# Attention beside a 2D Fourier filter on one core: queue order from an event simulation, exps over three and two PSUM banks in turn

## The chip, the cores and the metric

One core of one Trainium2 chip. The metric is the device time in microseconds of one execution; the time shown for a kernel is the median of several runs.

## The reference

Two independent parts share an input shape of 2048 x 640 and are written side by side (2048 x 1280, bf16).

Part A: a 2D real FFT of `A_x`, multiplied by a complex filter, and transformed back.

Part B: multi-head attention with 32 heads of 20 columns each:

```python
qkv = (x @ wqkv).reshape(B, S, 3, H, Dh).transpose(2, 0, 3, 1, 4)   # H = 32, Dh = 20
p = softmax(einsum("bhqd,bhkd->bhqk", q, k) * Dh ** -0.5)
o = einsum("bhqk,bhkd->bhqd", p, v).transpose(...).reshape(B, S, D) @ wo
```

## The kernel before, in words

**Tiles.** A head has only 20 columns, so four heads are packed on TensorE: a group `g` of four heads (8 groups) and a query block `qc` of 512 rows (4 blocks) make one of 32 units. A unit has 16 key chunks of 128 rows x 4 heads = 64 score tiles of 128 x 512; all 32 units have 2048. A score tile is one matmul with 20 contraction rows (`emit_qk`, L1550); up to four such matmuls run side by side in the rows of the array. ScalarE then takes the exponential of several tiles in one instruction, from PSUM to SBUF in bf16 (`emit_exp`, L1560). The result multiplies V with a column of ones appended (21 columns per head, `emit_pv`, L1589), and the four heads of a unit accumulate side by side in PSUM bank 6; the ones column gives the softmax denominators.

**PSUM.** Banks 0 to 2 and 3 to 5 are two halves of three tiles each. One exp reads a half (1536 columns) while TensorE fills the other. Bank 6 is the accumulator, bank 7 the single bank for all other work.

**Unit end** (`unit_done`). VectorE copies bank 6 to SBUF (L1603), four DMAs spread the denominators (L359 is the helper for all DMAs, issued by SyncE), VectorE takes the reciprocal (L1609), one DMA writes it to DRAM, one reads it back broadcast to all partitions, and GpSimd multiplies (L1615). When the eight units of a query block are done, eight out-projection jobs of eight matmuls each follow (L1633).

**Background jobs.** Part A is a chain of small matmul stages (L1115, L1148, L1168, L1192, L1224, L1288, L1314), with a pointwise stage on GpSimd (L1253 to L1258). The K projection (L1481), Q projection (`job_QA`, L1503) and V projection (L582) belong to part B. Each job is a run of matmuls into one PSUM bank and one evacuation to SBUF (L226 on VectorE, L225 on ScalarE; ScalarE evacuates only until the first scores).

**Order.** The engines take their instructions in program order, and a planner writes that order. `run` walks through steps of `T_STEP` = 1440 ns. Each step emits one exp, one score group of three tiles, one PV group of up to four tiles, and background matmuls for what is left of the step:

```python
budget = T_STEP - 250.0 * n_qk - 80.0 * n_pv - 150.0
banks = [7]
```

All costs are those of TensorE at its full clock. `unit_done` queues the whole unit end at once, the reciprocal directly behind the copy and the normalize behind it; the out-projection becomes due eight steps later.

Of the kernel before, what the change touches and what calls it, by code (L numbers as in the profile page):

```python
# [263 lines left out]
class KB:  # L264
# [805 lines left out]
    def mk_jobs_A(self, p0_after):  # L1070
# [205 lines left out]
        for lt in range(3):  # L1276
            M = 128 if lt < 2 else 65
            for sp in range(8):
# [16 lines left out]
                ev = [(mkev, 490.0, 598.0, [], [("ZT", lt, sp)] + zw("C", 2), [])]  # L1295
# [54 lines left out]
T_STEP = 1440.0  # L1350


class FK(KB):

# [5 lines left out]
    def alloc(self):  # L1360
# [22 lines left out]
        self.rin = [a.f32(take(64), 16) for _ in range(2)]  # L1383
        self.rall = a.f32(take(2048), 512)
# [5 lines left out]
        self.kron = a.bf(take(768), 3 * 128).rearrange("p (m k) -> p m k", m=3)  # L1390
        self.ws = self.osb[1].bitcast(BF16)[:, 0:656]
        self.zone(off[0], total)

    def zone(self, z, total):
# [9 lines left out]
        zA, zB, zC, zK = self.zA, self.zB, self.zC, self.zK  # L1404
        self.Wn = a.bf(zA, 2 * 16 * 328).rearrange("p (c k l) -> p c k l", c=2, k=16)
# [18 lines left out]
    def setup_B(self):  # L1424
        P = self.P
        nc = self.nc
# [4 lines left out]
        self.dma(self.xBn[:, 0:4, :], xB[:, 0:4, :], w=[("xBn", 0)], name="ld_xB0")  # L1431
        self.dma(self.wqkv[:, :, 640:720], wv[:, :, 640:720], w=[("wqkv", "k0")], name="ld_wk0")
        self.dma(self.wqkv[:, :, 0:80], wv[:, :, 0:80], w=[("wqkv", "q0")], name="ld_wq0")
        self.dma(self.xBn[:, 4:8, :], xB[:, 4:8, :], w=[("xBn", 1)], name="ld_xB1")
        self.dma(self.wqkv[:, :, 1280:1920], wv[:, :, 1280:1920], w=[("wqkv", 1)], name="ld_wv")
        for i in range(2, 4):
            self.dma(self.xBn[:, 4 * i:4 * i + 4, :], xB[:, 4 * i:4 * i + 4, :], w=[("xBn", i)], name="ld_xB%d" % i)
        self.dma(self.wqkv[:, :, 720:1280], wv[:, :, 720:1280], w=[("wqkv", "k")], name="ld_wk")
        self.dma(self.wqkv[:, :, 80:640], wv[:, :, 80:640], w=[("wqkv", "q")], name="ld_wq")
        wq, wk = self.wq_pad, self.wk_pad  # L1440
        ws = self.ws
        P.add("dve", lambda e: e.memset(ws, 0.25), w=[("ws",), ("osb", 1)], name="ms_ws")
        P.add("act", lambda e: e.activation(ws[:, 640:648], ws[:, 0:8], AF.Exp), r=[("ws",), ("osb", 1)], w=[("ws2",)], name="act_warm")
# [8 lines left out]
        wo = self.wo_pad.rearrange("p g n -> p (g n)")  # L1452
        P.add("pool", lambda e: e.memset(wo, 0.0), w=[("woz",)], name="ms_wo")
        o1 = self.ones1
        P.add("pool", lambda e: e.memset(o1, 1.0), w=[("ones1",)], name="ms_ones")
        wod = self.B_wo.rearrange("(g j d) n -> j d g n", g=8, j=4)
        for j in range(4):
            self.dma(self.wo_pad[32 * j:32 * j + 20, :, :], wod[j], r=[("woz",)], pw=[("wo",)], name="ld_wo%d" % j)
        for g in range(NG):
            for which, dst, key in ((1, wk, "wk"), (0, wq, "wq")):  # L1460
# [4 lines left out]
                if g < 1:  # L1465
                    P.add("act", (lambda d4, src: lambda e: e.copy(d4, src))(d4, src), r=[skey] + zk, w=[(key, g)], name="wpad")
                else:
                    P.add("pool", (lambda d4, src: lambda e: e.tensor_copy(d4, src))(d4, src), r=[skey] + zk, w=[(key, g)], name="wpad")

    def mk_jobs_B_static(self):  # L1470
        jobs = KB.mk_jobs_B_static(self)
        for g in range(NG):
            for kc in range(4):
                pe = []
                for cbv in range(5):
                    def mk(bank, cbv=cbv, g=g, kc=kc):
                        o = self.ps[:, bank, :]
# [5 lines left out]
                jobs[("K", g, kc)].pe = pe  # L1483
        return jobs

    def dummy(self, bank, n=512):
        ps = self.ps
        l = self.ws[:, 0:128]
        r_ = self.ws[:, 128:128 + n]
        self.P.add("pe", lambda e: e.matmul(ps[:, bank, 0:n], l, r_, start=True, stop=True),  # L1490
                   r=[("ws",), ("osb", 1)], w=[("ps", bank)], name="dummy")

    def job_QA(self, u):
# [17 lines left out]
        cond = (lambda p, u=u: self.qk_unit > u - 2) if u >= 2 else None  # L1511
        return Job("QA%d" % u, 2.0 + 32.0 * u - 6.0, pe, ev, after=[self.sj[("xT", qc, gi)] for gi in range(3)], cond=cond)


    def tile_of(self, t):
        u, w = divmod(t, 64)
        kt, j = divmod(w, 4)
        qc, g = divmod(u, NG)
        return u, qc, g, kt, j

    def group(self, i):
        return range(3 * i, min(3 * i + 3, self.ntiles))

    def qk_ready(self, p, i):
        for t in self.group(i):
            u, qc, g, kt, j = self.tile_of(t)
            for J in (self.qa_jobs.get(u), self.sj[("K", g, kt // 4)]):
                if J is None or J.done_p is None or J.done_p > p:
                    return False
        h = i % 2  # L1530
        for J in self.inflight:
            if J.bank in (3 * h, 3 * h + 1, 3 * h + 2):
                return False
        return True

    def emit_qk(self, i):
        ps, kt_ = self.ps, self.KT
        tiles, rk, wk = [], [], []
        for n, t in enumerate(self.group(i)):
            u, qc, g, kt, j = self.tile_of(t)  # L1540
            bank = 3 * (i % 2) + n
            tiles.append((j, g, kt, self.QA[u % 2], bank))
            rk += [("QA", u % 2), ("KT", g, kt // 4)]
            wk.append(("ps", bank))
            self.qk_unit = u
# [17 lines left out]
    def emit_pv(self, p):  # L1563
# [19 lines left out]
        if not tiles:  # L1583
            return 0
# [266 lines left out]
```

## Time and profile before

| | us |
|---|---|
| median of three runs (1208.11 to 1226.37) | 1223.77 |
| the profiled execution, its own time | 1226.82 |
| its span, first to last instruction | 1225.0 |
| ScalarE busy, 78% of the span | 951.9 |
| TensorE busy, 83% of the span | 1014.8 |
| VectorE busy, 20% | 246.0 |
| GpSimd busy, 11% | 137.6 |

PE is TensorE, PEld its weight loads, ACT ScalarE, DVE VectorE, POOL GpSimd, SPq the queue of SyncE. Busy time counts an instruction from its start to its modelled end; neighbours overlap, so the distance between starts says more than a mean duration. PEclk is the granted clock of TensorE: 1.00 is 2.4 GHz, 0.50 is 1.2 GHz, and a value between them is a mean over a stretch that had both.

### The profile page before, as it was taken

How to read it: one execution, taken by the hardware profiler on the slowest of the kernel's cores; microseconds unless marked ns; L12 is line 12 of the kernel's file. 1: busy time of each engine (PE TensorE's matmuls, PEld its weight loads, DVE VectorE, ACT ScalarE, POOL GpSimd, SP SyncE). 2: the span in 40 equal slices, each digit the busy share in tenths (PEclk: the TensorE clock that was granted, in tenths of full speed). 3: DMA queues.
4: the chain of work that ended last, by engine and by line, in shares of the span. 5: the costliest groups of instructions: out<-in, count | busy, mean ns of one | idle time of the engine just before them, and what ended most of it. 6: DMA issues, size and time to landing. Idle time of an engine off the chain costs nothing.

```text
span 1225.0 us, 13302 instructions
## 1 busy us (share of the span) xinstructions
PE 1014.8 (83%) x5818; PEld 291.8 (24%) x5864; DVE 246.0 (20%) x439; ACT 951.9 (78%) x689; POOL 137.6 (11%) x123
## 2 busy tenths in 40 slices
PE   7888888988869988897888788988888868888884
PEld 3322322223323212211112222223211211111112
DVE  3222333113212222331111233112100100000002
ACT  3678897977777977877778676757999869999990
POOL 4000001100000000273533000000000000000000
PEclk7788997557888666856557766559655755556556
DMA  6000003030000100000002000101000000000001
GB/s 194 1 10 11 9 1 99 10 123 10 10 26 6 62 10 10 1 10 10 10 8 88 15 10 2 40 31 52 23 10 10 25 15 10 10 10 10 10 10 33
DMA packets 30664, 31.85 MB, mean 26 GB/s; under 512 B 12936, under 2 KB 25864, under 8 KB 30216
## 3 DMA queue, kind: packets, MB, share of 16 engines
q1 hardware_dynamic: 30600, 30.94, 8.0%
q8 instruction: 47, 0.77, 0.3%
q14 instruction: 17, 0.14, 0.0%
HBM read 25.16 MB, written 5.51 MB: 25 GB/s over the span
## 4 chain that ended last, share of the span: by engine, by line
PE 52%; ACT 30%; DVE 6%; DMA 6%; SPq 3%; issue 2%; POOL 1%
ACT arena L1560 30%; PE ps L1550 12%; PE ps L1589 11%; DVE arena L226 4%; PE ps L1633 4%; PE ps L1503 4%; PE ps L1481 4%; PE ps L1314 3%; SPq L359 3%; DMA arena<-arena 3%; PE ps L1168 2%; PE ps L1224 2%; PE ps L582 2%; DMA arena<-rscr 2%; PE ps L1288 2%
## 5 line engine op out<-in xcount | busy, mean ns | idle before, releaser
L1560 ACT ACTIVATE arena<-ps 128x1536 bf16<-128x1536 f32 (+1 forms) x683 | 947.7, 1497 | 234.4 <-PE ps L1550 209.0
L1550 PE MATMUL ps<-arena 20*128 20x512 bf16 x2048 | 357.6, 517 | 61.2 <-ACT arena L1560 57.7
L1589 PE MATMUL ps<-arena 128*21 128x512 bf16 x2048 | 356.4, 517 | 5.6 <-DVE arena L1603 1.9
L226 DVE CAST arena<-ps 128x320 bf16<-128x320 f32 (+4 forms) x291 | 167.0, 574 | 623.6 <-PE ps L1503 167.1
L1615 POOL TENSOR_TENSOR arena<-arena 128x512 bf16<-128x512 f32 x32 | 40.5, 1265 | 1037.5 <-DMA arena<-rscr 1037.5
L1550 PEld LDWEIGHTS ps<-arena 20*128 20x128 bf16 x2048 | 69.7, 96 | 350.0 <-ACT arena L1560 217.0
L1589 PEld LDWEIGHTS ps<-arena 128*21 128x21 bf16 x2048 | 66.7, 91 | 249.2 <-issue 232.3
L1633 PE MATMUL ps<-arena 128*128 128x320 bf16 x256 | 52.7, 346 | 46.0 <-POOL arena L1615 45.5
L1481 PE MATMUL ps<-arena 128*128 128x512 bf16 x149 | 51.6, 451 | 19.6 <-DVE arena L226 17.0
L1503 PE MATMUL ps<-arena 128*128 128x512 bf16 x135 | 55.3, 511 | 7.7 <-issue 6.5
L226 DVE COPY arena<-ps 128x1024 bf16<-128x1024 bf16 (+2 forms) x57 | 35.5, 623 | 89.8 <-PE ps L1115 64.7
L1603 DVE COPY arena<-ps 128x512 f32<-128x512 f32 x32 | 22.1, 692 | 140.8 <-PE ps L1589 140.5
L1224 PE MATMUL ps<-arena 128*128 128x512 bf16 (+1 forms) x78 | 33.6, 514 | 20.0 <-DVE arena L226 14.1
L1314 PE MATMUL ps<-arena 128*128 128x320 bf16 (+1 forms) x192 | 43.0, 374 | 7.5 <-DVE arena L226 7.5
L1633 PEld LDWEIGHTS ps<-arena 128*128 128x128 bf16 x256 | 23.5, 108 | 70.1 <-issue 31.4
L1115 PE MATMUL ps<-arena 128*128 128x128 bf16 x246 | 27.2, 271 | 13.5 <-DVE arena L226 12.2
L1168 PE MATMUL ps<-arena 128*128 128x328 bf16 x160 | 29.7, 319 | 3.8 <-DVE arena L226 3.4
L1609 DVE RECIPROCAL arena<-arena 128x16 f32<-128x16 f32 x32 | 8.1, 253 | 118.3 <-DMA arena<-arena 118.3
L582 PE MATMUL ps<-arena 128*128 128x320 bf16 x160 | 29.8, 321 | 0.8 <-DVE arena L226 0.8
L1288 PE MATMUL ps<-arena 128*128 128x256 bf16 (+1 forms) x96 | 24.2, 405 | 3.9 <-DVE arena L226 3.7
L1192 PE MATMUL ps<-arena 128*128 128x328 bf16 x64 | 23.0, 463 | 3.9 <-DVE arena L226 3.8
L1314 PEld LDWEIGHTS ps<-arena 128*128 128x128 bf16 (+1 forms) x192 | 19.4, 115 | 27.5 <-DVE arena L226 17.3
(50 smaller groups left out, 258.2 us busy)
## 6 DMA issues: line engine op xcount, KB each, us to landing
arena<-rscr SPq DMA_DIRECT2D x32, 256.0 KB
arena<-in_B_x_dram SPq DMA_DIRECT2D x4, 640.0 KB, 7.0
arena<-in_A_x_dram SPq DMA_DIRECT2D x1, 2560.0 KB, 11.7
out_dram<-arena SPq DMA_DIRECT2D x16, 160.0 KB, 1.8
out_dram<-arena SPq DMA_DIRECT2D x4, 640.0 KB, 3.2
arena<-arena SPq DMA_DIRECT2D x128, 2.0 KB, 1.7
arena<-f_ciCS SPq DMA_DIRECT2D x1, 2048.0 KB, 8.7
arena<-f_cslab SPq DMA_DIRECT2D x1, 1536.0 KB, 6.1
```

What stands on the lines that cost most here:

```text
L226: return eng.tensor_copy(out, in_)
L582: return lambda e: e.matmul(o, l, r_, start=st, stop=sp)
L1168: return lambda e: e.matmul(o, l, r_, start=s_, stop=e_)
L1224: return lambda e: e.matmul(o, l, r_, start=s_, stop=e_)
L1288: return lambda e: e.matmul(o, l, r_, start=s_, stop=e_)
L1314: return lambda e: e.matmul(o, l, r_, start=s_, stop=e_)
L1481: return lambda e: e.matmul(o, l, r_, start=st, stop=sp)
L1503: return lambda e: e.matmul(o, l, r_, start=st, stop=sp)
L1550: inst = e.matmul(ps[:, bank, :], kt_[32 * j:32 * j + 20, g, kt * 128:(kt + 1) * 128], q[32 * j:32 * j + 20, :], start=True, stop=True, ti ...
L1560: self.P.add("act", lambda e: e.activation(pt, in_, AF.Exp, scale=SCALE), r=[("ps", h + k) for k in range(n)], w=[("PT", i % 4)], name="exp")
L1589: inst = e.matmul(ps[32 * j:32 * j + 21, 6, :], va[:, kt, h, :], pt, start=(kt == 0), stop=(kt == 15), tile_position=(0, 32 * j))
L1633: return lambda e: e.matmul(o, l, r_, start=st, stop=sp)
```

## The change

The planner by steps is replaced by an event simulation of the four engines in nanoseconds. Whenever an engine of the simulation is free, it takes the first thing that is possible at that moment, and that is written into its queue. Each instruction occupies its engine for a written-in duration, again that of TensorE's full clock (doubled in the first 12 us); a result counts as there 60 ns after the end, a matmul's 170 ns later still, and a change between score, PV and full matmuls adds 90 ns. The order of preference on TensorE is: score group, PV group, a chunk of background, a dummy matmul.

The other parts:
- 2048 tiles are dealt to exps of three and two tiles in turn; halves are banks 0 to 2 and 3 to 4. Banks 7 and 5 serve background jobs.
- A PV group needs four ready tiles of four different heads (or what is left of the unit).
- The unit end is queued in pieces: the copy when the last PV group is done and the normalize of the unit before is out; the reciprocal 2.5 us after the copy; the two scratch DMAs 2.2 us apart; the normalize 2.4 us after the second; the out-projection when the block's last normalize is done in the simulation. There is one copy buffer and one denominator buffer instead of two each. Maximum and minimum of the denominators are taken per unit (two small reduces), not over all reciprocals at the end.
- The V projection is cut in three parts of 80, 240 and 320 columns, so that the first heads' V is early; the loads are cut and ordered to match, and the output weights are loaded at 40 us.
- ScalarE evacuates background jobs until 45 us of the simulation when it has no exp, and after the last exp.
- If TensorE was planned to be busy for under 45% of the last 3 us, a dummy matmul is queued.
- A path for exponentials as powers on GpSimd is written, but the number of tiles given to it is zero (`NOFF`).

The core of the diff:

```diff
-T_STEP = 1440.0
+SEM = 60.0
+PE_LAT = 170.0
+MODE = 90.0
+DMA_NS = 2200.0
...
-        self.PT = [a.bf(take(3072), 1536) for _ in range(4)]
-        self.osb = [a.f32(take(2048), 512) for _ in range(2)]
+        self.PT = [a.bf(take(3072 - 1024 * (i % 2)), 1536 - 512 * (i % 2)) for i in range(4)]
+        self.osb = a.f32(take(2048), 512)
...
+    def occupy(self, e, dur, lat=0.0):
+        self.tf[e] = self.now + dur
+        self.log[e].append((self.now, dur))
+        self.at(self.now + dur)
+        t = self.now + dur + lat + SEM
+        self.at(t)
+        return t
...
+    def try_exp(self):
+        i = self.nexp
+        if i >= self.nqk or self.qk_t[i] > self.now or self.pt_free[i % 4] > self.now:
+            return False
...
+        t = self.occupy("act", 512 * n * 0.8333 + 97.0, 0.0)
+        self.half_free[i % 2] = t
...
+    def unit_copy(self, u):
+        P, ps, osb, rin = self.P, self.ps, self.osb, self.rin
+        P.add("dve", lambda e: e.tensor_copy(osb, ps[:, 6, :]), r=[("ps", 6)], w=[("osb",)], name="osb")
+        t = self.occupy("dve", 623.0)
+        self.ps6_free = t
...
+            self.dve_urgent.append((self.now + DMA_NS + 300.0, lambda: self.unit_recip(u)))
...
+            self.pool_q.append((self.now + DMA_NS + 200.0, lambda: self.unit_norm(u), lambda: self.op_left[:u // NG].count(0) == u // NG))
...
+    def bg_bank(self, job=False):
+        banks = [7, 5]
...
+    def warm(self):
...
+        if sum(d for _, d in h) > self.cfg["WARM_SHARE"] * 3000.0:
+            return False
...
+    def dispatch(self, e):
+        if e == "pe":
+            return (self.try_qk() or self.try_off_qk() or self.try_pv(4) or self.try_bg_pe() or self.warm())
+        if e == "act":
+            if self.try_exp():
+                return True
+            if self.nexp == 0 or (self.now < 45000.0 and self.nexp == self.nqk) or self.nexp == len(self.groups):
+                return self.try_bg_ev("act")
+            return False
+        if e == "dve":
+            return self.dve_q(self.dve_urgent) or self.try_off_copy() or self.try_bg_ev("dve") or self.vmax()
+        return self.dve_q(self.pool_q) or self.try_pow()
...
+        while acts:
+            n = 3 - len(self.groups) % 2
+            self.groups.append(acts[:n])
+            acts = acts[n:]
...
-    fast = FK(nc, arena, *args)
+    fast = FK(nc, arena, *args, cfg=dict(NOFF=lambda u: 0, T_POW=20000.0, WARM_SHARE=0.45))
```

## Rows read from the trace of the kernel before

**Rows 1.** Page, part 1: busy us, share of the span, instructions

```profile
PE 1014.8 (83%) x5818; PEld 291.8 (24%) x5864; DVE 246.0 (20%) x439; ACT 951.9 (78%) x689; POOL 137.6 (11%) x123
```

**Rows 2.** Windows by stage; columns as in the first line

```profile
core 0: us, PE busy (x) PEld busy (x) DVE busy (x) ACT busy (x) POOL busy (x), PEclk, DMA share, GB/s
0.00:50.00 50.00, 38.38 (x216) 16.24 (x219) 14.20 (x24) 18.16 (x17) 15.12 (x22) 0.73 0.41 119
50.00:875.00 825.00, 701.40 (x4132) 213.85 (x4164) 206.13 (x360) 638.99 (x456) 108.52 (x90) 0.72 0.08 26
...
1000.00:1190.00 190.00, 160.13 (x845) 30.71 (x850) 8.75 (x17) 185.21 (x138) 7.59 (x6) 0.54 0.03 10
```

**Rows 3.** Groups by form: busy us, mean ns | idle before it, releasers

```profile
L1560 ACT ACTIVATE arena<-ps 128x1536 bf16<-128x1536 f32 x682 | 946.8, 1497 | 234.4 <-PE ps L1550 209.0 <-PE ps L1589 22.1
...
L225 ACT COPY arena<-ps 128x1024 bf16<-128x1024 bf16 x1 | 1.0, 1012 | 2.2 <-PE ps L537 2.2
...
L225 ACT CAST arena<-ps 128x512 bf16<-128x512 f32 x1 | 0.6, 586 | 0.9 <-PE ps L1481 0.9
```

**Rows 4.** Timeline of PE, 1185 to 1190 us: start, duration, what

```profile
1185.50 0.61 PE L1550 MATMUL ps<-arena 20*128 20x512 bf16 x3 [0.20 <-ACT arena L1560]
1186.04 0.61 PE L1589 MATMUL ps<-arena 128*21 128x512 bf16 x3
...
1189.53 0.61 PE L1550 MATMUL ps<-arena 20*128 20x512 bf16 x3 [0.20 <-ACT arena L1560]
```

**Rows 5.** Timeline of ACT, first and last exps

```profile
13.93 5.48 ACT L1560 ACTIVATE arena<-ps 128x1536 bf16<-128x1536 f32 x4 [1.68 <-PE ps L1550]
...
1183.59 10.83 ACT L1560 ACTIVATE arena<-ps 128x1536 bf16<-128x1536 f32 x8
```

**Rows 6.** Timeline of all engines, 108 to 116 us: a unit's end

```profile
107.90 2.46 SPq L359 DMA_DIRECT2D arena<-arena  x4
...
111.57 0.25 DVE L1609 RECIPROCAL arena<-arena 128x16 f32<-128x16 f32 x1 [3.69 <-DMA arena<-arena]
...
114.47 1.45 ACT L1560 ACTIVATE arena<-ps 128x1536 bf16<-128x1536 f32 x1 [4.81 <-PE ps L1550]
```

**Rows 7.** Timeline of ACT, 840 to 860 us: the stage's last unit's end

```profile
853.93 1.45 ACT L1560 ACTIVATE arena<-ps 128x1536 bf16<-128x1536 f32 x1 [4.94 <-PE ps L1550]
```

**Rows 8.** Timeline of all engines, 358 to 376 us: a query block's end

```profile
363.46 0.58 SPq L359 DMA_DIRECT2D arena<-rscr  x1
368.43 1.26 POOL L1615 TENSOR_TENSOR arena<-arena 128x512 bf16<-128x512 f32 x1 [34.29 <-DMA arena<-rscr]
...
372.18 1.45 ACT L1560 ACTIVATE arena<-ps 128x1536 bf16<-128x1536 f32 x1 [12.07 <-PE ps L1550]
```

**Rows 9.** Timeline of PE, 58 to 62 us: steps at 2.4 GHz

```profile
58.69 0.39 PE L1550 MATMUL ps<-arena 20*128 20x512 bf16 x3
59.01 0.39 PE L1589 MATMUL ps<-arena 128*21 128x512 bf16 x3
...
60.13 0.39 PE L1550 MATMUL ps<-arena 20*128 20x512 bf16 x3
```

**Rows 10.** Timeline of all engines, 735 to 742 us: steps at 1.2 GHz

```profile
736.25 0.61 PE L1550 MATMUL ps<-arena 20*128 20x512 bf16 x3
...
736.90 1.45 ACT L1560 ACTIVATE arena<-ps 128x1536 bf16<-128x1536 f32 x1 [0.59 <-PE ps L1550]
...
738.29 0.61 PE L1550 MATMUL ps<-arena 20*128 20x512 bf16 x3
```

**Rows 11.** Timeline of all engines, 0 to 60 us: a group and its exp

```profile
54.05 0.39 PE L1550 MATMUL ps<-arena 20*128 20x512 bf16 x3
...
54.48 1.45 ACT L1560 ACTIVATE arena<-ps 128x1536 bf16<-128x1536 f32 x1 [0.31 <-PE ps L1550]
```

**Rows 12.** Windows of stretches with background, one at either clock

```profile
43.00:77.00 34.00, 28.55 (x206) 10.67 (x206) 9.63 (x18) 28.13 (x21) 0.00 (x0) 1.00 0.01 1
...
725.00:750.00 25.00, 25.00 (x125) 8.02 (x123) 8.30 (x12) 17.85 (x13) 0.00 (x0) 0.50 0.00 1
```

**Rows 13.** DMA issues: KB each, median us to landing

```profile
arena<-in_A_x_dram SPq DMA_DIRECT2D x1, 2560.0 KB, 11.7
```

More of the change, by code (lines that the diff above doesn't have):

```diff
@@ L1 @@
 import contextlib
+import heapq
 import math
@@ L1382, in alloc @@
         self.outB = [a.bf(take(1280), 640) for _ in range(2)]
-        self.rin = [a.f32(take(64), 16) for _ in range(2)]
-        self.rall = a.f32(take(2048), 512)
+        self.rin = a.f32(take(64), 16)
+        self.rc = a.f32(take(64), 16)
+        self.mm = a.f32(take(256), 64)
         self.cert = a.f32(take(32), 8)
@@ L1484, in mk_jobs_B_static @@
+        for k in [k for k in jobs if k[0] == "V"]:
+            del jobs[k]
+        jobs.update(V)
+        self.sj = jobs
         return jobs
@@ L1510, in job_QA @@
         ev = [(mkev, 490.0, 598.0, [], [("QA", u % 2)], [])]
[L1511 to L1532, printed above, removed]
-                return False
+        cond = (lambda p, u=u: self.qk_left[u - 2] == 0) if u >= 2 else None
@@ new lines, in job_QA, with done, at @@
+        return Job("QA%d" % u, 0.0, pe, ev, after=[self.sj[("xT", qc, gi)] for gi in range(3)], cond=cond,
+                   minp=(0.0 if u == 0 else 21000.0))
+    def done(self, J):
+        return J is not None and J.done_p is not None and J.done_p <= self.now
+    def at(self, t, fn=None):
+        self.seq += 1
+        heapq.heappush(self.events, (t, self.seq, fn))
+    def occupy(self, e, dur, lat=0.0):
[5 more added lines that the diff above has]
+        return t
@@ L1534, in qk_ready, with emit_qk @@
         return True
-    def emit_qk(self, i):
+    def emit_qk(self, tiles, banks):
         ps, kt_ = self.ps, self.KT
[L1538 to L1542, printed above, removed]
+        rk, mm = [], []
+        for (u, kt, j), bank in zip(tiles, banks):
+            qc, g = self.unit(u)
+            mm.append((j, g, kt, self.QA[u % 2], bank))
@@ new lines, in bg_bank @@
+    def bg_bank(self, job=False):
+        banks = [7, 5]
+        if job:
+            if not self.att:
+                banks += [0, 1, 2, 3, 4]
+            if self.u_pv == 0 and self.pv_left[0] == 64:
+                banks += [6]
+            if self.nexp == len(self.groups):
+                banks += [0, 1, 2, 3, 4]
+        for b in banks:
+            if self.bank_own.get(b) is None and self.bank_t.get(b, 0.0) <= self.now:
+                if b < 5 and self.att and self.half_free[b // 3] > self.now:
+                    continue
+                return b
+        return None
@@ new lines, in dve_q, with vmax @@
+    def dve_q(self, q):
+        for x in q:
+            if x[0] <= self.now and (len(x) < 3 or x[2]()):
+                q.remove(x)
+                x[1]()
+                return True
+        return False
+    def vmax(self):
+        kt = self.nvm
+        if kt >= 16 or not all(self.done(self.sj[("V", kt, part)]) for part in range(3)):
+            return False
+        self.nvm += 1
+        o = self.vmx[:, kt:kt + 1]
+        in_ = self.Vaug[:, kt, :, :].rearrange("p h e -> p (h e)")
+        self.P.add("dve", lambda e: e.tensor_reduce(o, in_, AX.X, ALU.max, apply_absolute_value=True),
+                   r=[("V", kt, 0), ("V", kt, 1), ("V", kt, 2), ("Vones",)], pw=[("vmx",)], name="vmax")
+        self.occupy("dve", 800.0)
+        return True
@@ new lines, in warm @@
+    def warm(self):
+        if not self.att or self.nexp >= len(self.groups):
+            return False
+        h = self.pe_hist
+        while h and h[0][0] < self.now - 3000.0:
+            h.pop(0)
+        if sum(d for _, d in h) > self.cfg["WARM_SHARE"] * 3000.0:
+            return False
+        bank = self.bg_bank()
+        if bank is None:
+            return False
+        self.dummy2(bank)
+        self.bank_t[bank] = self.occupy("pe", self.pe_dur(216.0, "f"))
+        return True
```

616 lines of the change are left out of this document (411 added, 205 removed).

## Prediction

> **What bounds the kernel now.** First the page's busy shares: PE 83%, ACT 78% [rows 1]. Neither is full, so I cut the run into stages [rows 2]. From 1000 to 1190 us ACT works 185.21 of 190 us: there the exps are the bound. From 50 to 875 us, where the background jobs (part A and the K, V and Q projections) are queued, it works 638.99 of 825 us. ACT's exps hold 947.7 us in all and stood idle 234.4 us, mostly waiting for the score matmuls of L1550 [rows 3]. So the exps are the floor, and PE, which has enough total time, delivers them late.
>
> The floor: where nothing disturbs ACT, score groups start at 1185.50 and, three exps on, at 1189.53 [rows 4], 1.343 us each; 683 of them are 917 us. The first exp starts at 13.93 us and the last ends at 1183.59 + 10.83 = 1194.4 us [rows 5], so 30.6 us follow it. 13.9 + 917 + 30.6 = 961.5; the span is 1225.0, so 263 us are lost between exps. Where:
> - 0 to 50 us: about 10.5 exps, 36.1 - 14.1 = 22 us lost [rows 2].
> - 50 to 875 us: 455 exps x 1.343 = 611, so 214 us lost. Two kinds of stop can be read in it. At a unit's end VectorE stands 3.69 us at the reciprocal, until the four denominator DMAs land; an evacuation is queued behind it, PE's next background job needs that bank, the score group is behind that job, and ACT idles 4.81 us. The last such stop of the stage has 4.94 us [rows 6, 7]. I count 15 at about 4.1: 62 us. At the end of a query block PE meets the out-projection before the normalize is there: 12.07 us of ACT [rows 8]; there are four blocks, two of whose ends lie in this stage: 24 us. The other 128 us are ordinary steps: a step hands PE 1440 ns of work, planned at the high clock. With TensorE at 2.4 GHz groups follow at 58.69 and 60.13 [rows 9], 1.44 us, 0.1 over the floor; at 1.2 GHz they follow at 736.25 and 738.29 [rows 10], 2.04 us, 0.7 over.
> - 875 us to the last exp: 319.4 - 217 x 1.343 = 28 us, of which one block end is 13.
>
> **The change part by part.**
>
> *Exps over 3 and 2 banks.* 2048 tiles are 410 exps of three and 409 of two. For 512 fewer columns ACT's own copies show 1012 - 586 = 426 ns [rows 3], so a two-bank exp takes 1.343 - 0.426 = 0.917 us (bounds: 0.895, two thirds, and 1.012, the lone copy). 410 x 1.343 + 409 x 0.917 = 926 us, 9 more than now. The Trainium skill (ScalarE: Activation LUTs, What ACT_TABLE_LOAD costs) has 186 ns + 0.833 ns per element, with 93 ns of overlap back to back; that makes 1.373 us for three banks, where the trace has 1.343, and an estimate of 950 us for the new exps, which would put the sum at 1104. The sum goes by the rows.
>
> *The margin behind a two-bank exp.* A score group is issued when the exp that frees its banks ends, and must be done when the other half's exp ends. From its start to its exp's start is 736.25 to 736.90 = 0.65 us at 1.2 GHz and 54.05 to 54.48 = 0.43 us at 2.4 GHz [rows 10, 11], plus about 0.1 of semaphore. Behind 0.917 us this leaves 0.17 and 0.39 us. A PV group already running takes 0.54 us at 1.2 GHz (1185.50 to 1186.04) and 0.32 us at 2.4 GHz [rows 4, 9]. So at 2.4 GHz it fits; at 1.2 GHz up to 0.37 us of every pair is lost, 0 to 150 us if it were so throughout.
>
> *PE's amount of work.* Score groups rise from 683 to 819; PV groups fall from some 683 of three to about 512 of four, since a PV group now waits for four different heads. 1331 groups x 0.32 = 426 us at 2.4 GHz, x 0.54 = 719 at 1.2. The background matmuls have some 550,000 columns by the code: 229 or 459 us, and some 500 entries into a run at 0.1 us: 50. Together 705 us, or 1228 us. With f the share of time at 2.4 GHz PE needs 1228/(1 + 0.74 f); at f = 0.44 (clock 0.72, the stage 50 to 875 [rows 2]) that is 927, as much as ACT. The new dummies come on top (none to some eight per unit by the 45% rule); below nothing where they raise the clock.
>
> *Background order and two banks.* Scores go first, background chunks of at most 0.22 us at 2.4 GHz fill holes, and with a second bank PE need not wait for one evacuation. At 2.4 GHz a pair of exps (2.26 us) holds 3.25 attention groups (1.04 us) and 1.2 us of background: the 0.1 us per exp goes. At 1.2 GHz the same queue takes 1.76 + 2.2 = 3.95 us, a loss of 1.7 per pair. The 170 us of background that are left after the start (part A, K, V) need some 140 pairs, so the dense stage should end near 400 us and not 875. Stretch 43 to 77 us had clock 1.00, 725 to 750 had 0.50 with PE busy for 25.00 of 25.00 us [rows 12], so I take the level as open and price both. Bounds: no pair at 1.2 GHz, 0 us; 56% of them as in that stage now, 133 us. I take 17%, 40 us, nearer to the dense stretch, in place of the 128.
>
> *Unit ends.* The reciprocal is queued 2.5 us after the copy ends; the DMAs took 3.7. VectorE still stands 1.2 us, mostly inside one exp of slack: 15 x 1.2 = 18 us for 62 (bounds 0 and 62). The normalize is queued 2.4 us after its DMA is issued and that took 368.43 - 363.46 = 5.0 [rows 8]; with the 1.2 the out-projection is some 3 us early, of which seven matmuls hide 1: 3 x 3 = 9 us for 37. The Trainium skill (DMA: Bandwidth & Descriptors, Anatomy of one DMA) has 2.0 us plus bytes for a DMA of POOL's path: by it the queue's 2.2 us would be enough, both terms nothing and the sum 1053. The rows of SyncE's DMAs say otherwise. SyncE issues the four DMAs in 2.46 us as now [rows 6], and what stands behind them in its queue (stores, part A's loads) is not due. One copy buffer instead of two is hidden: the next copy waits for the normalize, 12 us after this one, and units are 28 us apart. Two small reduces per unit lie on a VectorE that is 20% busy [rows 1].
>
> *Start.* First exp as now, at 13.9 (its loads stay first). The V weights of the first heads are split off and unit 0 no longer needs all 640 columns; ACT helps evacuate. I take 12 us lost for 22 (bounds 5 and 22). Part A's input is taken as landed 9.6 us after issue and needed 11.7 [rows 13]: 2 us once, inside the 40. Removed pow work: none is issued.
>
> *Late stage.* With little background PE needs 1.76 us of 2.26 at 1.2 GHz, plus projections and dummies; it loses 15 us in 319 now. Over 570 us with the thinner margin: 30 us (10 to 80).
>
> *Tail.* The same chain of DMAs and 64 matmuls: 31 us.
>
> Sum: 13.9 + 926 + (12 + 18 + 9 + 40 + 30) + 31 = 1080; the profiled run's time is 1.8 over its span, and 3.0 over the median of the runs. 1079, said as 1080.
>
> **The rivals.**
> - *PE is the bound, at 1.2 GHz* (slower): for it, the 25 full microseconds at 0.50 and the fixed order, which planned every group at 2.4 GHz; against it, 0.72 now with thinner work. Price: 14 + 1228 + 31 + 20 of unit ends = 1293. It decides from the point where 1228/(1 + 0.74 f) + 65 passes 1225: f under 0.08.
> - *Everything hidden*: the clock stays high in the dense stage, each unit's DMAs have landed when their readers come up: losses of 25, 13.9 + 926 + 25 + 31 = 996, as 995. For it, the stretch at 1.00 [rows 12]; against it, the DMA times. The Trainium skill's page on DMA (same section) speaks for its second half.
> - *The order drifts*: unit and block ends improve as above, but the 128 us and the start stay, because the plan's times and PE's part at the low clock: 22 + 18 + 9 + 128 + 50 = 227, and 14 + 926 + 227 + 31 = 1198 at the worst; with half of the 128 and of the late loss back, 1150. For it: a static order cannot see the clock.
> - *It does not do what it says*: the ends wait as before, for DMAs longer than planned, and PE's steps are no shorter: 1226 + 9 = 1235.
>
> **How the numbers follow.** Forecast 0.52 (its own range 1040 to 1120), everything hidden 0.14, order drifts 0.20, no effect 0.05, PE-bound 0.09. Faster 0.52 + 0.14 + 0.20 = 0.86, same 0.05, slower 0.09; 2%, 24 us, is about what this measurement can tell from no change. The range takes in most of hidden and of drift: 1005 to 1190.
>
> **What would show it.** Right: exps 410 and 409 with 0.92 us between starts in the short ones; reciprocal idle near 1.2 us per unit instead of 3.7; out-projection waits under 4 us; part A over by 450 us; ACT over 90% busy after 60 us. Wrong: a clock under 0.6 before 400 us with PE full, or idle of ACT under L1550 still above 150 us.

## The result and the profile after

| | before | after |
|---|---|---|
| median of four runs | 1224.99 us | 1106.25 us (1091.67 to 1120.71) |
| profiled execution | 1226.82 us, span 1225.0 | 1114.18 us, span 1112.0 |
| mean granted clock of it | 0.679 | 0.703 |

The ratio is 0.898, with a 95% interval of 0.880 to 0.916: faster, by some 119 us at the medians. Ratios with an interval, here and below, leave out runs over 1.5% above their kernel's fastest, so they can stand a little under the ratio of the medians. The forecast was 1080 us with a range of 1005 to 1190.

The page after, part 1 and the ACT and PEclk lines of part 2 (40 slices of 27.8 us):

```profile
PE 1043.3 (94%) x6131; PEld 301.4 (27%) x6131; DVE 244.9 (22%) x496; ACT 962.3 (87%) x836; POOL 137.8 (12%) x124
...
ACT  7999998798689988896699988998898898888991
...
PEclk9999988796599955795599555555558555555556
```

PE went from 83% [rows 1] to 94% and ACT from 78% to 87%. The clock line has two parts: mostly full speed, with holes, in the first 22 slices (to some 610 us), and 0.5 nearly throughout behind them.

Groups by form of the kernel after (L1678 are the exps, L1804 the reciprocal, L1845 the out-projection):

```profile
L1678 ACT ACTIVATE arena<-ps 128x1536 bf16<-128x1536 f32 x410 | 597.3, 1457 | 109.8 <-PE ps L1768 54.2 <-PE ps L1661 53.4
...
L1678 ACT ACTIVATE arena<-ps 128x1024 bf16<-128x1024 f32 x409 | 421.5, 1031 | 7.5 <-PE ps L1661 7.0
...
L1845 PE MATMUL ps<-arena 128*128 128x320 bf16 x256 | 53.4, 352 | 10.3 <-POOL arena L1825 10.3
...
L1804 DVE RECIPROCAL arena<-arena 128x16 f32<-128x16 f32 x32 | 8.1, 253 | 75.8 <-DMA arena<-arena 75.7
```

The idle time before exps is halved, from 234.4 us [rows 3] to 117.3. Of that, 109.8 us lie before three-bank exps, each of which follows a two-bank one, and 7.5 before two-bank exps. Half of the 109.8 is put down not to a score group but to a PV group (L1768). The out-projection waits for a normalize only once, 10.3 us, in the tail. VectorE still idles 75.8 / 32 = 2.4 us per unit before the reciprocal.

Windows by stage of the kernel after; columns as in [rows 2]:

```profile
50.00:150.00 100.00, 99.68 (x691) 34.37 (x689) 47.51 (x86) 95.62 (x84) 4.74 (x4) 1.00 0.04 12
500.00:550.00 50.00, 49.20 (x212) 14.42 (x213) 8.13 (x18) 31.49 (x27) 1.26 (x1) 0.50 0.06 19
550.00:600.00 50.00, 49.69 (x376) 20.02 (x373) 14.50 (x33) 47.47 (x41) 1.27 (x1) 0.99 0.14 47
600.00:1083.00 483.00, 452.40 (x2201) 93.20 (x2197) 29.37 (x81) 438.36 (x379) 19.00 (x15) 0.54 0.04 12
```

The same view over the whole dense stage:

```profile
50.00:600.00 550.00, 531.36 (x3459) 179.78 (x3456) 197.62 (x375) 477.93 (x411) 102.40 (x85) 0.82 0.11 35
```

With 926 / 819 = 1.131 us an exp, the 411 exps from 50 to 600 us are 465 us of work: 85 lost. The 379 from 600 to 1083 us are 428: 55 lost. The 29 before 50 us take 36 us from the first exp on, 3 over their 33. So 143 us are lost between exps, where the forecast had 109.

Both kinds of step stand in the traces. At 1.2 GHz, 519 to 526 us (timeline of PE and ACT; start, duration):

```profile
519.99 0.61 PE L1661 MATMUL ps<-arena 20*128 20x512 bf16 x3
...
520.54 1.25 PE L1315 MATMUL ps<-arena 128*128 128x320 bf16 x4
520.65 1.45 ACT L1678 ACTIVATE arena<-ps 128x1536 bf16<-128x1536 f32 x1 [1.29 <-PE ps L1661]
521.71 0.61 PE L1661 MATMUL ps<-arena 20*128 20x512 bf16 x2
...
522.36 1.02 ACT L1678 ACTIVATE arena<-ps 128x1024 bf16<-128x1024 f32 x1 [0.26 <-PE ps L1661]
522.79 1.51 PE L1315 MATMUL ps<-arena 128*128 128x320 bf16 x5
524.24 0.61 PE L1661 MATMUL ps<-arena 20*128 20x512 bf16 x3
...
524.90 1.45 ACT L1678 ACTIVATE arena<-ps 128x1536 bf16<-128x1536 f32 x1 [1.51 <-PE ps L1661]
```

Three-bank exps start at 520.65 and 524.90: 4.25 us a pair, 2.0 over the 2.26 of the floor. This pair is among the longer ones: the whole window of 500 to 550 us, at 0.50, holds 27 exps, 3.7 us a pair and 1.4 over the floor. The background matmuls that the plan fitted behind an exp (1.25 and 1.51 us here) stand ahead of the next score group. At the full clock, and at a unit's end, 106 to 112 us:

```profile
106.77 0.69 DVE L1789 COPY arena<-ps 128x512 f32<-128x512 f32 x1
...
107.48 2.43 SPq L360 DMA_DIRECT2D arena<-arena  x4
...
109.16 3.71 ACT L1678 ACTIVATE arena<-ps 128x1536 bf16<-128x1536 f32 x3 [0.36 <-PE ps L1768]
...
111.09 0.25 DVE L1804 RECIPROCAL arena<-arena 128x16 f32<-128x16 f32 x1 [2.04 <-DMA arena<-arena]
```

Here VectorE stands 2.04 us and ACT runs on: three exps in 3.71 us, which less the last (1.45) is 2.26 a pair, the floor as forecast. In [rows 6] the same place cost ACT 4.81 us.

### The profile page after: what moved, and what is told of

The parts are those of the page before. It is cut to its first block, busy times and chain, and to the rows that moved or that the text cites. A ratio compares the mean times of both kernels' runs of the same rounds, so it can differ in the third digit from the quotient of the medians.

```text
span 1112.0 us, 14252 instructions
## 1 busy us (share of the span) xinstructions
PE 1043.3 (94%) x6131; PEld 301.4 (27%) x6131; DVE 244.9 (22%) x496; ACT 962.3 (87%) x836; POOL 137.8 (12%) x124
## 4 chain that ended last, share of the span: by engine, by line
PE 76%; ACT 18%; DMA 1%; POOL 1%; issue 1%; DVE 1%; SPq 1%; POOLq 0%
PE ps L1661 27%; ACT arena L1678 17%; PE ps L1768 16%; PE ps L1572 8%; PE ps L1585 5%; PE ps L1845 4%; PE ps L1315 3%; PE ps L1509 3%; PE ps L1169 2%; PE ps L1547 2%; PE ps L1225 2%; PE ps L1193 1%; DMA arena<-arena 1%; SPq L360 1%; PE ps L1149 1%
## 5 line engine op out<-in xcount | busy, mean ns | idle before, releaser
L1678 ACT ACTIVATE arena<-ps 128x1536 bf16<-128x1536 f32 (+1 forms) x819 | 952.3, 1244 | 117.3 <-PE ps L1661 60.4
L1661 PE MATMUL ps<-arena 20*128 20x512 bf16 x2048 | 417.2, 505 | 43.5 <-ACT arena L1678 41.1
L227 DVE CAST arena<-ps 128x512 bf16<-128x512 f32 (+5 forms) x286 | 163.8, 573 | 651.2 <-PE ps L1585 362.1
L1768 PE MATMUL ps<-arena 128*21 128x512 bf16 x2048 | 263.5, 506 | 2.1 <-ACT arena L1678 1.0
L1661 PEld LDWEIGHTS ps<-arena 20*128 20x128 bf16 x2048 | 81.8, 95 | 351.6 <-ACT arena L1678 252.0
L1572 PE MATMUL ps<-arena 128*128 128x512 bf16 x187 | 109.5, 587 | 0.0
L1768 PEld LDWEIGHTS ps<-arena 128*21 128x21 bf16 x2048 | 51.4, 91 | 178.8 <-issue 171.9
L1585 PE MATMUL ps<-arena 128*128 128x512 bf16 x160 | 64.9, 518 | 0.0
L1845 PE MATMUL ps<-arena 128*128 128x320 bf16 x256 | 53.4, 352 | 10.3 <-POOL arena L1825 10.3
L1509 PE MATMUL ps<-arena 128*128 128x512 bf16 x160 | 46.3, 383 | 0.3 <-ACT arena L226 0.3
L1572 PEld LDWEIGHTS ps<-arena 128*128 128x128 bf16 x187 | 19.2, 103 | 77.4 <-issue 77.0
L1845 PEld LDWEIGHTS ps<-arena 128*128 128x128 bf16 x256 | 25.1, 110 | 35.0 <-issue 12.5
L1169 PE MATMUL ps<-arena 128*128 128x328 bf16 x160 | 30.5, 311 | 0.4 <-DVE arena L227 0.4
L1547 PE MATMUL ps<-arena 128*128 128x240 bf16 (+1 forms) x160 | 26.8, 285 | 0.3 <-DVE arena L227 0.3
L1804 DVE RECIPROCAL arena<-arena 128x16 f32<-128x16 f32 x32 | 8.1, 253 | 75.8 <-DMA arena<-arena 75.7
L1585 PEld LDWEIGHTS ps<-arena 128*128 128x128 bf16 x160 | 14.7, 112 | 30.2 <-issue 26.9
```

The costliest lines, as they stand in the source:

```text
L227: return eng.tensor_copy(out, in_)
L1169: return lambda e: e.matmul(o, l, r_, start=s_, stop=e_)
L1509: return lambda e: e.matmul(o, l, r_, start=st, stop=sp)
L1547: return lambda e: e.matmul(o, l, r_, start=st, stop=sp)
L1572: self.P.add("pe", lambda e: e.matmul(ps[:, bank, 0:512], k[:, 0, 0:128], k[:, 0, 0:512], start=True, stop=True), r=[("KT", 0, 0)], w=[("p ...
L1585: return lambda e: e.matmul(o, l, r_, start=st, stop=sp)
```

## The experiments

All start from the kernel before or after; nothing of the computation is left out in any (e3 and e7 leave out dummy matmuls). Each was timed beside the kernel before on the same chip.

**b1_defer: the unit ends alone.** The kernel before, old planner, with only the unit end cut in two: copy and denominator DMAs as before, the rest (reciprocal, scratch DMAs, normalize) queued three steps later. The out-projection jobs become due as before.

```diff
+        self.later.append((p + 3, lambda: self.unit_rest(u)))
+        if g == NG - 1:
+            self.jobs_outproj(qc, p + 8)
+
+    def unit_rest(self, u):
...
         P.add("dve", lambda e: e.reciprocal(r16, rin), r=[("rin", b2)], w=[("rall", u)], name="recip")
...
-        self.unit_p[u] = p
-        if g == NG - 1:
-            self.jobs_outproj(qc, p + 8)
...
+            while self.later and self.later[0][0] <= p:
+                self.later.pop(0)[1]()
```

> The kernel before with one thing changed: at a unit's end the copy and the four DMAs are queued as now, the reciprocal, the scratch DMAs and the normalize three steps (4.3 us) later. Theory A (the wait of VectorE at the reciprocal is behind the stops of about 4.1 us at 15 unit ends): the stops go, 50 to 65 us, 1160 to 1175 us, 0.95 to 0.96 of before. Rival C (the stops have another cause, or the time is lost again in steps that TensorE is late with anyway): 1205 to 1225 us, 0.985 to 1.0.

Measured: 1061.23 us, 0.877 (0.868 to 0.885). That is some 155 us for a move of a few lines, and more than the whole change brings. The idle time before exps falls from 234.4 us [rows 3] to 72.1, and the out-projection waits for a normalize only in the tail:

```profile
L1560 ACT ACTIVATE arena<-ps 128x1536 bf16<-128x1536 f32 x682 | 936.4, 1526 | 72.1 <-PE ps L1550 47.7 <-PE ps L1589 20.1
...
L1639 PE MATMUL ps<-arena 128*128 128x320 bf16 x256 | 48.9, 328 | 10.8 <-POOL arena L1624 10.2 <-DVE arena L226 0.6
```

Its unit end, 100 to 105 us:

```profile
100.14 0.69 DVE L1603 COPY arena<-ps 128x512 f32<-128x512 f32 x1 [1.78 <-PE ps L1589]
...
100.86 2.46 SPq L359 DMA_DIRECT2D arena<-arena  x4
...
103.53 0.69 DVE L226 CAST arena<-ps 128x512 bf16<-128x512 f32 x1 [2.10 <-PE ps L1481]
...
104.52 0.25 DVE L1618 RECIPROCAL arena<-arena 128x16 f32<-128x16 f32 x1 [0.30 <-DMA arena<-arena]
```

The evacuation at 103.53 passes ahead of the reciprocal, which then waits 0.30 us. The direct price of the stops was 62 us of unit ends and 37 of block ends by the forecast's own count; b1 gave 56 us more than both. Where they come from is seen around the stop in the kernel before (windows: ahead of it, behind it, after that):

```profile
84.00:107.00 23.00, 21.20 (x139) 6.50 (x141) 5.53 (x8) 22.47 (x17) 1.27 (x1) 1.00 0.01 1
112.00:118.00 6.00, 5.58 (x22) 1.40 (x22) 1.05 (x2) 2.90 (x2) 0.00 (x0) 0.50 0.14 45
118.00:145.00 27.00, 26.69 (x200) 10.55 (x199) 10.01 (x19) 26.15 (x19) 1.27 (x1) 1.00 0.01 1
```

The granted clock is 1.00 until the stop, 0.50 for the 6 us that follow it (two exps in them, where 27 us at 1.00 hold 19), and 1.00 again. A stop is paid twice: for itself, and in slow steps behind it. Over a longer stretch, the kernel before and then b1:

```profile
400.00:600.00 200.00, 171.51 (x891) 40.27 (x899) 53.87 (x94) 155.32 (x111) 55.45 (x47) 0.63 0.05 16
```

```profile
400.00:600.00 200.00, 173.04 (x1183) 50.79 (x1197) 61.30 (x103) 188.08 (x140) 80.25 (x72) 0.83 0.07 23
```

PE is busy for as long, at 0.83 and not 0.63, and does a third more in it.

**b2_step: a shorter step on top.** b1 with less planned PE work per step.

```diff
-T_STEP = 1440.0
+T_STEP = 1350.0
```

> The kernel before with the unit ends queued three steps later (1061 us) and with the planner's step shortened from 1440 to 1350 ns, the distance of two exps, so that a step holds less background. Theory G (a step that is 0.1 us longer than an exp costs that in each of some 400 steps at 2.4 GHz): 20 to 40 us faster, 1020 to 1040 us, 0.84 to 0.855 of before. Rival H (background is then only stretched over more steps, and the sparser TensorE runs more at 1.2 GHz): 1055 to 1090 us.

Measured: 1051.22 us, 0.869 (0.864 to 0.873). By the ratios that is some 10 us more than b1, between the two expectations, but the intervals overlap. With the stops gone, the 0.1 us by which a step passes the floor is at most a small term.

**e2_recip_at_once: the same part undone in the change.** The reciprocal is queued when its DMAs are issued; the read-back, the normalize and the out-projection keep their times.

```diff
-            self.dve_urgent.append((self.now + DMA_NS + 300.0, lambda: self.unit_recip(u)))
+            self.dve_urgent.append((self.now + 0.0, lambda: self.unit_recip(u)))
...
-            self.at(self.now + DMA_NS, d2)
+            self.at(self.now + 4700.0, d2)
```

> The changed kernel with the reciprocal queued on VectorE directly behind the unit's copy, as before the change; the scratch DMAs, the normalize and the out-projection are queued at the same simulated times as in the changed kernel. Theory A (this wait of some 3.7 us was worth about 4 us of ScalarE at each of 15 unit ends in the stage with background): 25 to 50 us slower than the changed kernel, 1125 to 1150 us, 0.92 to 0.94 of before. Rival C (with two background banks and scores first, TensorE rides over a VectorE that stands for 3.7 us): within 10 us of the changed kernel, 0.89 to 0.91.

Measured: 1186.48 us, 0.966 (0.959 to 0.973), clock 0.661. Against the change's 0.898 that is 0.068 of 1217, about 80 us. The rival that a second bank hides the wait falls, and my 25 to 50 was too small. A unit end of it, 148 to 152 us:

```profile
148.23 0.40 PE L1768 MATMUL ps<-arena 128*21 128x512 bf16 x4
149.44 0.25 DVE L1804 RECIPROCAL arena<-arena 128x16 f32<-128x16 f32 x1 [3.62 <-DMA arena<-arena]
...
150.45 0.94 PE L1509 MATMUL ps<-arena 128*128 128x512 bf16 x3 [1.82 <-DVE arena L227]
...
151.32 0.61 PE L1661 MATMUL ps<-arena 20*128 20x512 bf16 x3
...
151.98 1.45 ACT L1678 ACTIVATE arena<-ps 128x1536 bf16<-128x1536 f32 x1 [2.23 <-PE ps L1661]
```

VectorE waits 3.62 us, PE 1.82 us for VectorE's evacuations, ACT 2.23 us. PE's groups take 0.40 us before the stop (2.4 GHz) and 0.61 behind it (1.2 GHz).

**e1_three: exps over three banks again.** The change with 3 + 3 banks for the halves, and P tiles (the exps' outputs in SBUF) of three banks' width; this leaves one bank for background, and the two can't be parted this way round, since the PV bank and two halves of three fill seven of eight.

```diff
-            n = 3 - len(self.groups) % 2
+            n = 3
...
-        banks = [7, 5]
+        banks = [7]
```

> The changed kernel with every exp over three banks (683 exps again) and, since banks 3 to 5 are the second half, one background bank (7); the simulated order stays. Theory A (what is left after the change is lost behind the two-bank exps, whose 0.915 us are too short for a score group at 1.2 GHz): the floor falls by 8 us, the 7 to 8 us per 50 us that are lost from 600 us on fall to under 2, so 1040 to 1075 us, 0.85 to 0.88 of the kernel before. Rival B (two background banks and the 3-and-2 rhythm carry the gain): background runs slower on one bank, TensorE waits for evacuations again, 1130 to 1190 us, 0.92 to 0.97.

Measured: 1063.14 us, 0.869 (0.862 to 0.876), clock 0.739. The 3-and-2 rhythm with its second bank is a loss of some 0.029 x 1217 = 35 us, not a gain. Of the 83.6 us that e1's three-bank exps still waited, 82.7 were for score groups.

**e4_one_bank: the 3-and-2 rhythm with one bank.** The second of e1's two lines alone.

> The changed kernel with its exps over 3 and 2 banks, but one background bank (7) as before; bank 5 is unused. Told apart: what the three-bank variant (1063 us) gained over the changed kernel, the rhythm of the exps or the number of background banks. Theory A (the rhythm: behind a two-bank exp a score group comes late): the second bank matters little, 1095 to 1125 us, 0.90 to 0.925 of before, as the changed kernel. Rival E (two interleaved background jobs break TensorE's runs up and so cost more than they give): with one bank as fast as the three-bank variant, 1055 to 1080 us.

Measured: 1201.0 us, 0.991 (0.985 to 0.997), clock 0.657. Both expectations missed by far. Within the rhythm the second bank is worth about 0.09 x 1208 = 112 us; with three-bank exps one bank was enough to beat the change (e1). A stretch of it, 620 to 623 us:

```profile
620.62 1.78 PE L1845 MATMUL ps<-arena 128*128 128x320 bf16 x6
620.73 1.02 ACT L1678 ACTIVATE arena<-ps 128x1024 bf16<-128x1024 f32 x1 [0.27 <-PE ps L1661]
...
622.34 0.61 PE L1661 MATMUL ps<-arena 20*128 20x512 bf16 x3
...
622.99 1.45 ACT L1678 ACTIVATE arena<-ps 128x1536 bf16<-128x1536 f32 x1 [1.24 <-PE ps L1661]
```

Six background matmuls, 1.78 us at 1.2 GHz, stand ahead of the next score group, beside an exp of 1.02 us. Part A ran until 888 us here and until 606 us in the change; why one bank costs that much is not taken apart further.

**e3_no_dummy and e7_early_dummy: the dummies.** e3 queues none; e7 only while background jobs other than Q projections and out-projections remain.

```diff
-    fast = FK(nc, arena, *args, cfg=dict(NOFF=lambda u: 0, T_POW=20000.0, WARM_SHARE=0.45))
+    fast = FK(nc, arena, *args, cfg=dict(NOFF=lambda u: 0, T_POW=20000.0, WARM_SHARE=-1.0))
```

```diff
+        if not any(J.pe and J.name[:2] not in ("QA", "OP") for J in self.jobs):
+            return False
```

> The changed kernel without its 187 dummy matmuls (158 of them after 600 us). Theory A (after 600 us TensorE ran at 1.2 GHz in spite of them, mean clock 0.54, so each is 0.54 us that a score group waits for): the late loss falls from about 60 to 30 us, 1065 to 1085 us, 0.87 to 0.885 of before. Rival D (they hold the clock up in part of the stage): the clock after 600 us falls to 0.50 and the time stays or rises, 1095 to 1130 us.

> The changed kernel with dummy matmuls only as long as jobs of part A or of the K and V projections are in the queue (29 or so of 187). Without any dummies the time was 0.918 of before, with all 0.898. Theory F (the few early ones keep the clock up in the stage with background, the late ones only take TensorE's time at 1.2 GHz): 1075 to 1095 us, 0.88 to 0.895, and two-bank intervals after 600 us back at their floor of 0.90. Rival D (it is the late ones that pay): 1110 to 1125 us, as with none.

Measured: e3 1117.79 us, 0.918 (0.913 to 0.924), clock 0.668; e7 1101.78 us, 0.895 (0.891 to 0.900), clock 0.684. By these ratios the dummies pay some 20 us, and the 29 early ones as much as all 187; by the medians (0.919 for e3, 0.912 for e7, 0.903 for the change) it is less. e7's runs took 1081, 1083, 1120 and 1124 us and e3's 1112 to 1139, so a gain from the early ones is not shown beyond the scatter. From 600 us on the dummies hold PE 94 us of the 452 busy (158 of them) in the kernel after, and taking these out changes nothing that can be measured.

**e5_dma_real and e6_three_dma: the traced DMA times.** The chain's three delays set to what the trace of before shows (denominators 3.7 us, scratch 1.5, read-back 5.0) in place of 2.5, 2.2 and 2.4; e5 on the change, e6 on e1.

```diff
-            self.dve_urgent.append((self.now + DMA_NS + 300.0, lambda: self.unit_recip(u)))
+            self.dve_urgent.append((self.now + 3700.0, lambda: self.unit_recip(u)))
...
-            self.at(self.now + DMA_NS, d2)
+            self.at(self.now + 1500.0, d2)
...
-            self.pool_q.append((self.now + DMA_NS + 200.0, ...
+            self.pool_q.append((self.now + 5000.0, ...
```

> The changed kernel, exps over 3 and 2 banks and two background banks, with only the unit end's times set to those in the trace (reciprocal 3.7 us after the copy, broadcast 1.5 us after the write, normalize 5.0 us after the broadcast). The same edit took the three-bank variant from 1063 to 1026 us. Theory A (a unit's end that is queued before its DMAs have landed stops VectorE, then TensorE, and leaves TensorE at 1.2 GHz, whatever the rhythm of the exps): 25 to 45 us faster than the changed kernel, 1055 to 1080 us, 0.87 to 0.89 of before. Rival E (two background banks already cover that wait): 1090 to 1110 us, as the changed kernel.

> The three-bank variant with the unit end queued at the times that the DMAs took in the trace: reciprocal 3.7 us after the copy (2.5 in the change), broadcast 1.5 us after the write (2.2), normalize 5.0 us after the broadcast (2.4). Theory A (VectorE still stands some 2.4 us at each reciprocal and that is still in the way of evacuations): the wait falls under 0.5 us per unit, and the time by 10 to 25 us to 1040 to 1055, 0.85 to 0.865 of before. Rival C (what is left of the wait is covered): 1055 to 1070 us, as the three-bank variant.

Measured: e5 1118.47 us, 0.919 (0.912 to 0.926); e6 1025.72 us against 1208.05, a ratio of medians of 0.849, too scattered (1003 to 1033) for an interval. With two banks the longer delays bring nothing, as the rival has it that the two banks cover VectorE's remaining wait, though 1118 lies above the rival's range too. Whether e5 is slower than the change at all stays open: the intervals overlap. With one bank they are worth some 30 us (e1 was 0.874 by its medians).

**e8_three_dma_warm: more dummies on e6.** WARM_SHARE 0.45 to 0.60.

> The three-bank variant with the unit end at the traced times (1026 us), and dummies queued whenever TensorE was planned busy for under 60% of 3 us (45% before). Theory F (dummies keep the clock at 2.4 GHz where background is thin, and this is worth more than the time they take): a mean clock over 0.80, losses from 350 to 700 us fall from 60 to 30 us, 990 to 1010 us, 0.82 to 0.835. Rival D (TensorE is full of dummies at 1.2 GHz): 1035 to 1070 us.

Measured: 1047.53 us, 0.857 (0.849 to 0.864), profiled at a clock of 0.813 where e6 had 0.768. A higher clock, and not faster: it seems that the dummies take the time that they buy.

**e9_three_dma_plan: a plan at a lower clock.** e6 with every planned PE duration 1.3 times as long, so that the order has room when the clock is low.

```diff
-        if self.now < 12000.0:
-            dur *= 2.0
+        dur *= 2.0 if self.now < 12000.0 else 1.3
```

> The three-bank variant with the unit end at the traced times (1026 us), and every TensorE duration in the simulation multiplied by 1.3, between the two clocks, so that less background is queued between two score groups. Theory I (what is left is lost where an order planned at 2.4 GHz runs at 1.2): at 1.2 GHz a score group then comes late by less, 1000 to 1015 us, 0.83 to 0.84. Rival H (the thinner order runs more at 1.2 GHz, and lasts longer): 1030 to 1060 us.

Measured: 1160.4 us, 0.956 (0.951 to 0.961), clock 0.613. The rival holds in its direction, and its 1030 to 1060 us was far too little. Windows of e9, then of the next kernel, whose plan differs in that factor alone:

```profile
50.00:600.00 550.00, 488.86 (x2900) 129.06 (x2928) 126.73 (x255) 475.52 (x344) 29.61 (x19) 0.70 0.08 24
...
600.00:1000.00 400.00, 385.83 (x1975) 91.36 (x1992) 88.78 (x170) 345.71 (x243) 86.51 (x77) 0.50 0.06 20
```

```profile
50.00:600.00 550.00, 485.14 (x3552) 161.32 (x3586) 187.60 (x356) 531.53 (x393) 105.43 (x88) 0.89 0.10 33
...
600.00:1000.00 400.00, 355.33 (x2000) 88.29 (x2024) 40.81 (x109) 362.60 (x267) 15.84 (x13) 0.62 0.06 18
```

From 50 to 600 us PE is busy equally long (489 and 485 us), at 0.70 with 2900 matmuls and at 0.89 with 3552; ACT gets 344 and 393 exps. The roomier order leaves background for the late stage (part A ends at 1124 us, and at 705 in the next kernel), which then runs at 0.50 throughout. That the thinner order is what lowered the clock is argued; the run shows that the two come together. The factor also counts in the rule for dummies, so 2 of them are left where the next kernel has 102; the loss without dummies in e3, some 20 us, is small beside the 144 us (0.119 x 1210) here.

**e10_three_dma_again: the best version, more rounds.** e6's kernel.

> The three-bank variant with the unit end at the traced times once more, in five rounds, since its first interval was missing and its times spread from 1003 to 1033 us. Theory A (unit ends at the traced times are worth some 25 to 35 us where one background bank waits for VectorE): 1005 to 1040 us, 0.835 to 0.86 of before, apart from the 0.862 to 0.876 of the three-bank variant with the change's times. Rival C (the first figure was the spread): 1045 to 1070 us, 0.865 to 0.875.

Measured: 1027.13 us (1002.54 to 1043.59) against 1206.35; 0.837 (0.830 to 0.844), and 0.851 by the medians. It beats the kernel after by some 0.05 to 0.06. Its groups by form:

```profile
L1678 ACT ACTIVATE arena<-ps 128x1536 bf16<-128x1536 f32 x682 | 925.9, 1651 | 45.3 <-PE ps L1661 44.6
...
L1804 DVE RECIPROCAL arena<-arena 128x16 f32<-128x16 f32 x32 | 8.0, 250 | 43.4 <-DMA arena<-arena 43.4
```

ACT's idle before exps is 45.3 us, of 117.3 in the change, and VectorE idles 1.4 us per unit before the reciprocal.

## Why the prediction was right, and where its terms were off

**The direction held, and the size in part by luck.** 1080 was forecast, 1106 measured. Of the gain of 144 us that the forecast had, 72 were unit and block ends (62 - 18 and 37 - 9) and 72 all the rest. The deferral alone gave 155 us in the kernel before (b1), and the change with all the rest stands 0.021 x 1217 = 26 us behind b1 (whose deferral is 4.3 us and not 2.5). A gain priced at half and a loss priced as a gain nearly made up for each other.

The frame (first exp, floor, losses, tail) stands: 410 and 409 exps, the pair at 2.26 us, first exp at 14.4, tail 28.4 us (the last exp ends at 1083.6) for 31. The losses came to 143 us for 109. The start lost 3 for 12. By the two-part cost that the Trainium skill has (ScalarE: Activation LUTs, What ACT_TABLE_LOAD costs) the pair would be 950 / 926 of the 2.26, an estimate of 2.32 us; the measured 2.26 decides.

**Unit ends: the mechanism right, its term too small.** The step "15 x 1.2 = 18 us for 62", a gain of 44, priced only ACT's stops. Undoing that part alone costs 80 us (e2). Doing the deferral alone in the kernel before gives 155 us (b1, the block ends included), where the forecast's prices for both were 62 and 37. The rest lay, at least in part, in "the other 128 us are ordinary steps": part of these were steps at 1.2 GHz that a stop had brought about, as in the 6 us at 0.50 behind the stop of [rows 6]. How much of the rest they make up is not shown.

The 1.2 us of reciprocal wait held, though the profile has 2.4. At the unit end of 107 us the copy ends at 107.46 and the reciprocal starts when the DMAs have landed, 3.63 us later. Queued 2.5 us behind the copy by the plan, it held VectorE's queue for 1.13 us; over all 32 units the mean is 1.15. The other 0.9 of the 2.04 us idle is time for which nothing was queued. In the late stage nothing stands between copy and reciprocal, so the whole wait counts as idle, though it holds nothing up (VectorE of the kernel after):

```profile
659.94 0.69 DVE L1789 COPY arena<-ps 128x512 f32<-128x512 f32 x1 [0.41 <-PE ps L1768]
664.26 0.25 DVE L1804 RECIPROCAL arena<-arena 128x16 f32<-128x16 f32 x1 [3.63 <-DMA arena<-arena]
```

The Trainium skill (DMA: Bandwidth & Descriptors, Anatomy of one DMA) gives 2.0 us plus bytes for POOL's path; by it the queue's times would have been enough and the sum 1053. For these four DMAs of SyncE the measurement decides: 3.63 us from the copy's end to the reciprocal. Longer delays bring 30 us where one bank is left (e6).

**Dense steps: the price of a pair about right, their number wrong.** "A loss of 1.7 per pair" measured 2.0 in the rows above and 1.4 over the whole window around them. I took 17% of 140 pairs, 24. The clock of 0.82 from 50 to 600 us means 36% of 550 us at 1.2 GHz, 198 us; at 4.25 us a pair these are 47 pairs and 94 us, at 3.7 us 53 pairs and 77 us. The 85 lost there lie between the two. "The dense stage should end near 400 us" failed for the same reason: part A ran to 606 us.

**The late stage** lost 55 us for 30. The bound stood in the text: up to 0.37 us of every pair at 1.2 GHz. About 190 pairs at a mean clock of 0.54 lost 55 / 190 = 0.29 each; I had priced it nearer to what the three-bank order loses.

**Block ends: nothing for 9, and my reading of before was wrong.** The 12.07 us of [rows 8] were not an out-projection waiting for its own block's last unit. Rows of the kernel before:

```profile
355.44 0.99 PE L1633 MATMUL ps<-arena 128*128 128x320 bf16 x6
...
369.84 1.76 PE L1633 MATMUL ps<-arena 128*128 128x320 bf16 x6 [11.58 <-POOL arena L1615]
```

Jobs of that block had run at 355.44; the last came after the normalize at 368.43 [rows 8], which is that of the next block's first unit and had been queued ahead of the job. Both blocks' rows lie in one tile (`OTn`), so this last job multiplied the next block's rows for four of the 32 heads. This is a fault in the order of the kernel before, in three of its four blocks, and not only lost time. In b1 and in the change the normalize stands behind the job. For that the change queues a block's normalize only when the earlier block's out-projection is out, and the wait is gone. The tail keeps its own:

```profile
1096.51 3.92 PE L1845 MATMUL ps<-arena 128*128 128x320 bf16 x14 [10.26 <-POOL arena L1825]
```

**Two edits had the wrong sign.** The exps over three and two banks were costed at 9 us of ACT, plus margin; they cost 35 together with the second bank (e1). Before three-bank exps lie 109.8 of the 117.3 us of idle, and two waits make them up. The score group behind a two-bank exp is late where PE runs at 1.2 GHz, as forecast. The other wait is in no term of the forecast: 88 three-bank exps, 54.2 us, waited last for a PV group, which stands behind the score group in PE's queue and still reads the P tile that the exp overwrites. At 515 to 519 us:

```profile
515.79 0.61 PE L1661 MATMUL ps<-arena 20*128 20x512 bf16 x3
516.33 0.61 PE L1768 MATMUL ps<-arena 128*21 128x512 bf16 x4
...
517.00 2.37 ACT L1678 ACTIVATE arena<-ps 128x1536 bf16<-128x1536 f32 x2 [2.10 <-PE ps L1768]
```

By such rows of all 88, some 32 us (an estimate, matmul ends being modelled) lie behind the end of the score group. With three-bank exps such waits are all but gone: in e10 44.6 of 45.3 us are for score groups. The second bank was counted as a gain of its own. At one bank the rhythm costs 0.122 x 1217 = 148 us (e4 against e1), and the second bank earns 112 of them back (e4 against the change). The dummies, counted as a cost or nothing, earn 20 us at most, and not clearly (e3, e7).

**The rivals and the signs.** The rival of a drifting order had the right cause in it (a fixed order at a clock it can't see). Its sum is wrong: 1198 with half of the 128 and of the late 50 back is 1109, not 1150, so by its own words it comes nearer to the 1112 us of the span than the 1080, though it kept 22 us at the start where 3 were lost. As for the others, the rival of a PE at 1.2 GHz came true only from 600 us on, at a mean of 0.54, where little background was left, and in stretches before. Planning for the low clock is no cure (e9).

Of the signs of being right, the counts of exps and the out-projection's waits came. ACT was busy 916 of 1033 us from 50 to 1083 us, 89% and not over 90, and part A was over at 606 us, not 450. One sign of being wrong came for a stretch, full PE at a clock under 0.6 before 400 us:

```profile
278.00:306.00 28.00, 28.00 (x125) 8.22 (x122) 6.46 (x13) 17.65 (x16) 1.26 (x1) 0.50 0.06 22
```

## What to carry to other kernels

In an in-order queue, queue the reader of a DMA when the DMA has landed by the trace, behind the work that others wait for: this one edit (b1) was worth more in the old planner than the whole change. Check as well that no work is queued behind a write that replaces what it still has to read. Price a stop of PE with the steps behind it at the lower clock, by a window on either side, and not by the idle time alone. An order planned at the full clock that runs late beat one with room in it (e10, e9), so try a change of plan on the chip before reasoning it out.

## What the runs showed of the hardware

- A full PE in the profile goes with either clock. From 500 to 550 us of the kernel after PE is busy 49.20 of 50 us at 0.50, in the next 50 us 49.69 at 0.99; the first holds 27 exps, the second 41.
- A unit end's stop was followed by 1.2 GHz: in the kernel before for 6 us, between stretches at 1.00, and in e2, where PE had idled 1.82 us, by groups of 0.61 us and not 0.40. What size of stop it takes, no run here measured.
- A higher mean clock is not a faster kernel: the profiled runs have 0.813 and 1037 us in e8, 0.785 and 1021 us in e10.
- One kernel's times scatter by several per cent where the clock goes to and fro: 1003 to 1044 us in e10 at a profiled 0.785, and 1159 to 1161 in e9, whose late stage is at 0.50 throughout. What puts a given stretch at the lower level stays open.
